# Four blocks of attention: VectorE's share of the exponentials in fewer passes and for more banks, and values without a tick of rest at unit ends

## The chip, the core and the metric

The kernel runs on one core of a Trainium2 chip. The metric is the device time of one execution in microseconds. Five engines take part, each with its own queue of instructions worked off in order: TensorE (PE in the profile, its weight loads PEld), VectorE (DVE), ScalarE (ACT), GpSimd (POOL) and SyncE (SP, which here issues DMAs). They wait for each other through semaphores. Matmuls write to PSUM, eight banks of 128 x 512 float32 values; everything else lies in SBUF or in DRAM.

## The reference

Four transformer blocks follow each other on one sequence of 2048 rows and 640 columns in bf16, with 32 heads of 20 columns. Blocks 1 and 3 use the weights A and a sliding window of 256 keys, causal; blocks 2 and 4 use the weights B and full attention over all 2048 keys, with no mask.

```python
def _B_ref(x, wqkv, wo):                     # full attention; _A_ref adds the window's mask
    qkv = (x @ wqkv) ...                     # 3 x (32 heads, 2048, 20)
    scores = einsum("bhqd,bhkd->bhqk", q, k) * (Dh ** -0.5)
    p = softmax(scores, axis=-1)
    o = einsum("bhqk,bhkd->bhqd", p, v)
    return o.transpose(...).reshape(B, S, D) @ wo

x = x + _A_ref(_layernorm(x), A_wqkv, A_wo)
x = x + _B_ref(_layernorm(x), B_wqkv, B_wo)
x = x + _A_ref(_layernorm(x), A_wqkv, A_wo)
x = x + _B_ref(_layernorm(x), B_wqkv, B_wo)
```

The two full blocks need 2 x 32 x 2048 x 2048 exponentials, the most numerous operation of the kernel.

## The kernel before

The code counts the layers l = 0 to 3. "Layer 2" is l = 1, the first full one; "the last layer" is l = 3.

**Units, banks, ticks.** The work on scores is cut into units: one layer l, one chunk c of 512 queries, one group g of four heads, and for c = 0 of a full layer a part of the keys. A unit of a full layer has 16 blocks of 128 keys for each of its four heads, that is 64 banks: a bank is the scores of one head, 128 keys by 512 queries, and fills one PSUM bank. The loop at the end of the kernel makes one tile of two to four banks in each tick `t`. A tick emits, in this order: the score matmuls of the tile (line 1222), ScalarE's exponential of the whole tile from PSUM to a bf16 tile `pt` in SBUF (line 1253), other work in portions (`pump`), filler matmuls where `keep_clock` finds TensorE too idle (line 613), the value matmuls of banks that were exponentiated two or three ticks earlier (line 1289), a portion of VectorE's own exponentials (`side_step`), and the masks of windowed tiles (line 1325). Even ticks write their scores to PSUM banks 0 to 2, odd ones to 3 to 5, or 3 to 6 when a tile has four banks. Bank 7 (`op`) collects the values of the unit, each of the four heads in 32 of its partitions, and with them the sum of the exponentials in a 21st column. Bank 6 (with 5 at first) is the one bank for all other matmuls: projections, transposes, the output product, the tails.

**Values at a unit's end.** Values are emitted in groups of four banks, one key block for four heads. When the last group of a unit is out, `finish_unit` (line 787) lets VectorE copy bank 7 to `oT` (lines 808 and 810) or to a partial sum `raw_o` (794 and 796); a tail in four steps then normalizes it. The first group of the next unit overwrites bank 7, so it has to wait for that copy. In the kernel before, line 1273 lets no values be emitted in the tick after a unit's end, and allows up to two groups in a later one.

**Exponentials on VectorE.** Some banks of the full layers do not go to ScalarE (`Unit.aside`, line 632): of the last key block, two heads of each unit in layer 2 and four in the last layer, from c = 1 on, with two units left out. VectorE works on them in pairs, by the generator `t_side` (lines 837 to 899). It reads each bank's scores from PSUM and turns them into an integer whose bits are those of 2 to the power of the score (line 858); it splits off the mantissa and the exponent (863, 868, 873), corrects the mantissa by a polynomial of the fourth degree (875 to 893) and multiplies the two (896). Each large pass has 1024 elements for 128 partitions, in float32. `side_step` emits the passes one by one against a credit of 0.65 a tick in layer 2 and 1.05 in the last layer (line 1310). In layer 2 the scores of such a bank take the place of a third bank in a tile, so that ScalarE gets two (line 1137); in the last layer they are an extra matmul to bank 6 (line 851). The values of the pairs are emitted when the unit ends (line 1298, after `side_done`). Intermediate tiles are borrowed: from `raw_o` in layer 2 (`side_early`), from the tiles of normalized inputs in the last layer (`side_start`).

**Other work.** Projections, layer norms, output products and tails are generators with a due unit; `choose` picks the next one and `pump` advances it by a credit of TensorE time. They write to bank 6, have it read by VectorE (line 304 for copies, 539, 995, 1008, 1020), and then give it free for the next tick. When the last layer's chunks c = 1 to 3 are on, only tails and output products are left.

Of the kernel before, what the change touches and what calls it, by code (L numbers as in the profile page):

```python
# [34 lines left out]
EK, ES, EB, EC, ED = (  # L35
    0.34108128280528366, -0.013389613744261132, 0.7155463694844106,
    0.9531181402314826, 0.010462897723623632,
)
# [11 lines left out]
def kernel(  # L50
# [571 lines left out]
    class Unit:  # L622
        def __init__(self, l, c, g, part=None):
# [5 lines left out]
            else:  # L629

                if c > 0 and (l, c, g) not in ((3, 1, 0), (3, NC - 1, G - 1)):
                    self.aside = (2, 3) if l == 1 else (0, 1, 2, 3)
# [3 lines left out]
                    if kc < NT - 1 or j not in self.aside  # L636
                ]
            n = len(sets)
# [179 lines left out]
    def side_start():  # L818

        assert live["xnT"] == 0  # L820
        tl = [xtp.tile([P, KD, C], BF16, name="xnT", tag="xnT") for _ in range(4)]
        live["xnT"] += 4
        f = [v[:, 0:4, :].rearrange("p a b -> p (a b)") for v in tl[0:3]]
        side["tiles"] = [v.bitcast(F32) for v in f] + [tl[3][:, 0:2, :].rearrange("p a b -> p (a b)")]
# [3 lines left out]
    def side_early():  # L828

        b = part_o["t"]  # L830
        side["tiles"] = [b[:, 2 * n : 2 * n + 2, :].rearrange("p a b -> p (a b)") for n in range(3)]
        side["tiles"].append(b[:, 6, :].bitcast(BF16))
        side["out"] = deque([b[:, 7, :].bitcast(BF16).rearrange("p (a b) -> p a b", a=2)])
        side["gen"] = t_side()
        side_step(False)

    def t_side():

        V = nc.vector
        while aside:  # L840
            u = aside[0]
            for pair in range(len(u.aside) // 2):
                while id(u) not in loaded or (u.l == 3 and not side["late"]):
                    yield None
                for i in range(2):
                    yield "bank"
                    xi, xm, xw, xe = side["tiles"]
                    if u.l == 3:
# [3 lines left out]
                            ps[:, 6, :], lhsT=u.k(NT - 1, u.aside[2 * pair + i]),  # L852
                            rhs=u.q(u.aside[2 * pair + i], 0, 4), start=True, stop=True,
# [6 lines left out]
                        scalar1=SCALE * LOG2E * E23, scalar2=127.0 * E23, op0=ALU.mult, op1=ALU.add,  # L860
# [3 lines left out]
                    out=xm.bitcast(I32), in0=xi.bitcast(I32), scalar1=0x7FFFFF, scalar2=0x3F800000,  # L864
# [4 lines left out]
                    out=xi.bitcast(I32), in0=xi.bitcast(I32), scalar1=-0x800000, scalar2=None,  # L869
                    op0=ALU.bitwise_and,  # L870
                )
                yield 0.7
                V.tensor_scalar(out=xe, in0=xi, scalar1=0.0, scalar2=None, op0=ALU.max)
                yield 0.7
                V.tensor_scalar(
                    out=xm, in0=xm, scalar1=EK, scalar2=ES, op0=ALU.mult, op1=ALU.add
                )
                yield 0.7
                V.tensor_tensor(out=xw, in0=xm, in1=xm, op=ALU.mult)
                yield 1.2  # L880
                V.tensor_scalar(out=xw, in0=xw, scalar1=EB, scalar2=None, op0=ALU.add)
                yield 0.7
                V.tensor_tensor(out=xw, in0=xw, in1=xw, op=ALU.mult)
                yield 1.2
                V.tensor_scalar(
                    out=xm, in0=xm, scalar1=EC, scalar2=ED, op0=ALU.mult, op1=ALU.add
                )
                yield 0.7
# [4 lines left out]
                V.tensor_tensor(out=po, in0=xw, in1=xm, op=ALU.add)  # L893
                yield 1.2

                V.tensor_tensor(out=po, in0=po, in1=xe, op=ALU.mult)
                side_out.setdefault(id(u), []).append(pt)
                yield 0.7
# [28 lines left out]
    def side_need(u):  # L927

        if u.l == 3:
            n = 0  # L930
            while u in aside and side.get("scored", {}).get(id(u), 0) < 4:
# [10 lines left out]

    def side_done(u):
        n = 0
        while len(side_out.get(id(u), ())) < len(u.aside) // 2:
# [3 lines left out]
            if side_step(mfree[6][0] <= state["tick"]):  # L949
                continue  # L950
            t = choose(False)
            if t is None:
                state["tick"] += 1
            else:
                advance(t)
        return side_out.pop(id(u))
# [409 lines left out]
```

## Time and profile before

| what | value |
|---|---|
| time, median of 3 runs | 2373.48 us (2369.16 to 2375.21) |
| profiled execution: its own time, its span | 2373.48 us, 2371.8 us |
| busy: TensorE, VectorE, ScalarE, GpSimd | 2015.1, 1459.4, 2183.9, 142.5 us |
| granted TensorE clock, mean | 0.803 |
| exponentials of line 1253 | 1641 activations, 2105.9 us busy |
| score matmuls of line 1222, full layers | 4008, 674.8 us busy |
| value matmuls of line 1289, full layers | 3860, 490.6 us busy |
| VectorE's first read of a bank (line 858) | 88 in the last layer, 48 in layer 2 |

The span is the time from the first to the last instruction. Busy time of an engine counts instructions that overlap once. A matmul's listed duration includes its way through the array, so four matmuls on separate rows or columns of the array, which run at once, are listed with nearly the same start. The names behind an arrow are tiles: `pt<-ps` reads PSUM and writes `pt`. In a table of waits a row gives who waited for whom, microseconds in total, how many times, and the longest.

### The profile page before, as it was taken

What the parts mean: (1) busy time and instruction counts of PE and PEld (TensorE: products, weight loads), DVE (VectorE), ACT (ScalarE), POOL (GpSimd) and SP (SyncE); (2) the same over time, 40 slices, a digit from 0 to 9 for tenths busy, and PEclk for the clock granted to TensorE, in tenths of its full rate; (3) what the DMA queues carried; (4) which work ended last, traced back from release to release, by engine and by line L of the source; (5) the groups of instructions that cost most, each with busy time, mean ns of one, the idle gap of its engine ahead of it and who ended that gap; (6) DMA issues with size and microseconds to landing.
All of it is one profiled execution on the core that took longest, in us unless ns stands there. A gap on an engine that the chain in (4) does not pass through costs nothing.

```text
span 2371.8 us, 39878 instructions
## 1 busy us (share of the span) xinstructions
PE 2015.1 (85%) x15408; PEld 708.8 (30%) x15554; DVE 1459.4 (62%) x2724; ACT 2183.9 (92%) x1753; POOL 142.5 (6%) x295
## 2 busy tenths in 40 slices
PE   7888998878888888888888888888888888888887
PEld 3443333323322332223322333232322222222222
DVE  7676776425646666566666554352577777777772
ACT  7787889898999998999999999999999999999997
POOL 3111110000000001000010011001000000000000
PEclk9998999987987998879997999798655565556556
DMA  6232422322300223102331034022111010001100
GB/s 183 73 101 65 113 68 58 83 62 64 82 19 27 57 54 104 39 14 54 75 89 37 1 87 118 28 42 71 53 32 39 26 38 26 26 26 38 39 14 12
DMA packets 173679, 132.53 MB, mean 56 GB/s; under 512 B 115761, under 2 KB 156081, under 8 KB 173489
## 3 DMA queue, kind: packets, MB, share of 16 engines
q1 hardware_dynamic: 163872, 101.39, 17.3%
q0 software_dynamic: 9616, 28.59, 3.5%
q8 instruction: 122, 2.00, 0.4%
q14 instruction: 69, 0.56, 0.1%
HBM read 98.70 MB, written 27.79 MB: 53 GB/s over the span
## 4 chain that ended last, share of the span: by engine, by line
ACT 35%; PE 33%; issue 14%; DVE 14%; DMA 2%; SPq 2%; POOL 0%; ACTq 0%; DVEq 0%; another core or an unknown queue 0%; POOLq 0%
ACT pt L1253 33%; PE ps L1222 9%; PE ps L1289 6%; PE ps L353 5%; PE ps L530 4%; DVE pt L1325 3%; PE ps L444 3%; PE ps L613 2%; DMA wqk<-in_B_wqkv_dram 1%; DVE st L304 1%; DVE on L1020 1%; ACT ka L1253 1%; DVE oT L810 1%; DVE raw_o L858 1%; PE ps L1016 1%
## 5 line engine op out<-in xcount | busy, mean ns | idle before, releaser
L1253 ACT ACTIVATE pt<-ps 128x1536 bf16<-128x1536 f32 (+2 forms) x1641 | 2105.9, 1451 | 143.6 <-PE ps L1222 129.2
L1222 PE MATMUL ps<-qt,kt 32*128 32x512 bf16 x4008 | 674.8, 480 | 201.9 <-ACT pt L1253 167.9
L1289 PE MATMUL ps<-pt,vt 128*21 128x512 bf16 x3860 | 490.6, 480 | 7.7 <-issue 5.2
L1222 PEld LDWEIGHTS <-kt 32*128 32x128 bf16 x4008 | 190.2, 94 | 648.4 <-issue 627.8
L1325 DVE TENSOR_TENSOR pt<-pt,masks 128x1024 bf16<-128x1024 bf16 (+5 forms) x403 | 239.1, 626 | 134.7 <-ACT pt L1253 134.1
L353 PE MATMUL ps<-xnT,wqk 128*128 128x512 bf16 x760 | 215.6, 395 | 33.2 <-DMA wqk<-in_B_wqkv_dram 11.5
L1289 PEld LDWEIGHTS <-vt 128*21 128x21 bf16 x3960 | 100.7, 91 | 338.5 <-issue 331.1
L304 DVE CAST st<-ps 128x512 bf16<-128x512 f32 x127 | 87.8, 691 | 169.3 <-PE ps L353 165.8
L613 PE MATMUL ps<-masks,ident 128*128 128x512 bf16 x474 | 176.7, 436 | 9.3 <-issue 3.3
L530 PE MATMUL ps<-wop,on 128*128 128x320 bf16 x976 | 171.7, 320 | 6.6 <-DVE on L1020 3.0
L1222 PE MATMUL ps<-qa,ka 32*128 32x384 bf16 (+2 forms) x1408 | 118.9, 279 | 36.1 <-ACT pt L1253 30.5
L858 DVE TENSOR_SCALAR xnT<-ps 128x512 int32<-128x512 f32 x88 | 60.8, 691 | 106.6 <-PE ps L851 103.8
L1020 DVE TENSOR_TENSOR on<-oT,ps 128x512 bf16<-128x512 bf16 x128 | 87.4, 683 | 61.0 <-PE ps L1016 59.6
L810 DVE CAST oT<-ps 128x512 bf16<-128x512 f32 x112 | 76.8, 686 | 73.5 <-PE ps L1289 47.8
L539 DVE TENSOR_TENSOR x_sb<-x_sb,ps 128x320 bf16<-128x320 bf16 x120 | 57.9, 482 | 102.9 <-PE ps L530 102.8
L444 PE MATMUL ps<-wv,xnT 128*128 128x320 bf16 x640 | 111.2, 307 | 8.2 <-DVE va L304 1.8
L530 PEld LDWEIGHTS <-on 128*128 128x128 bf16 x976 | 91.6, 103 | 75.8 <-issue 40.2
L353 PEld LDWEIGHTS <-wqk 128*128 128x128 bf16 x830 | 72.4, 99 | 126.4 <-issue 54.4
L1289 PE MATMUL ps<-pt,va 128*21 128x384 bf16 (+2 forms) x1408 | 81.2, 294 | 6.1 <-DVE pt L1325 2.1
L1222 PEld LDWEIGHTS <-ka 32*128 32x128 bf16 x1408 | 44.7, 92 | 104.4 <-issue 95.2
L444 PEld LDWEIGHTS <-xnT 128*128 128x128 bf16 x640 | 56.6, 99 | 50.3 <-issue 31.6
L1016 PE MATMUL ps<-rT,spread 32*128 32x128 bf16 x512 | 62.0, 254 | 5.2 <-DVE vs L304 2.1
(105 smaller groups left out, 1589.7 us busy)
## 6 DMA issues: line engine op xcount, KB each, us to landing
vt<-v_d SPq DMA_DIRECT2D x48, 336.0 KB
kt<-k_d SPq DMA_DIRECT2D x192, 80.0 KB
wqk<-in_B_wqkv_dram SPq DMA_DIRECT2D x80, 160.0 KB
wqk<-in_A_wqkv_dram SPq DMA_DIRECT2D x70, 160.0 KB
k_d<-st POOLq DMA_DIRECT2D x75, 128.0 KB, 2.2
q_d<-st POOLq DMA_DIRECT2D x75, 128.0 KB, 2.1
qt<-q_d SPq DMA_DIRECT2D x384, 20.0 KB
v_d<-vs POOLq DMA_DIRECT2D x16, 336.0 KB, 3.7
```

Source lines behind the costliest of these rows:

```text
L304: nc.vector.tensor_copy(out=out_, in_=in_)
L353: nc.tensor.matmul(pq, lhsT=wt[:, dc, :], rhs=xt[:, dc, :], start=(dc == 0), stop=(dc == KD - 1),)
L444: nc.tensor.matmul(pv, lhsT=xt[:, dc, i * P : (i + 1) * P], rhs=wv_sb[l % 2][:, dc, h * HD : (h + 1) * HD], start=(dc == 0), stop=(dc == K ...
L530: nc.tensor.matmul(yp, lhsT=on[:, g, qb * P : (qb + 1) * P], rhs=wop[:, g, i * HD : (i + 1) * HD], start=(g == g0), stop=(g == G - 1),)
L613: nc.tensor.matmul(ps[:, b, :], lhsT=ident[:], rhs=masks[:, 0, :], start=True, stop=True)
L810: nc.vector.tensor_copy(out=oT[:], in_=op)
L1016: nc.tensor.matmul(zb[:, qb * P : (qb + 1) * P], lhsT=spread4[:, qb, :], rhs=rT[:], start=True, stop=True,)
L1020: nc.vector.tensor_tensor(out=on[:, g, :], in0=oT[:], in1=zb, op=ALU.mult)
L1222: nc.tensor.matmul(sp[:, i, col * P : (col + qn) * P], lhsT=u.k(kc, j), rhs=u.q(j, q0, qn), start=True, stop=True,)
L1253: nc.scalar.activation(out=pt[:, i:k, b0 * P :], in_=sp[:, i:k, b0 * P :], func=ACT.Exp, scale=SCALE,)
L1289: nc.tensor.matmul(op[32 * j : 32 * j + VW, q0 * P : (q0 + qn) * P], lhsT=u.v(kc, j), rhs=pg[:, i, col * P : (col + qn) * P], start=(first ...
L1325: nc.vector.tensor_tensor(out=pt_[:, i:k, b0 * P :], in0=pt_[:, i:k, b0 * P :], in1=mv_, op=ALU.mult,)
```

## The change

A pair of VectorE's banks takes eight passes in place of twelve: the two reads from PSUM (now scaled and bounded below), two integer passes, and four passes that each do two operations with a second tensor (`scalar_tensor_tensor`), the last of which multiplies with the power of two. The polynomial is of the third degree. Each unit of layer 2 from c = 1 on gives four banks to VectorE instead of two; in the last layer units with an even g give four as before and those with an odd g six. The credit in layer 2 is 0.8 a tick. The values of a pair are emitted with a group of its unit's values, four ticks after the pair's last pass or at the unit's end. `side_step` is called before the values of a tick, not after them. The tick without values after a unit's end and the two groups in one tick are gone: every tick may emit one group. A four-bank tile may follow a use of bank 6 one tick of its kind earlier.

```diff
-                    self.aside = (2, 3) if l == 1 else (0, 1, 2, 3)
+                    self.aside = tuple((NT - 1, j) for j in range(4))
+                    if l == 3 and g % 2:
+                        self.aside += ((NT - 2, 0), (NT - 2, 1))
...
                     V.tensor_scalar(
                         out=xi.bitcast(I32)[:, i * C : (i + 1) * C], in0=side["psum"],
-                        scalar1=SCALE * LOG2E * E23, scalar2=127.0 * E23, op0=ALU.mult, op1=ALU.add,
+                        scalar1=SCALE * LOG2E * E23, scalar2=-128.0 * E23,
+                        op0=ALU.mult, op1=ALU.max,
                     )
                     yield 0.7
                 V.tensor_scalar(
-                    out=xm.bitcast(I32), in0=xi.bitcast(I32), scalar1=0x7FFFFF, scalar2=0x3F800000,
+                    out=xm.bitcast(I32), in0=xi.bitcast(I32), scalar1=0x7FFFFF, scalar2=0x3E800000,
                     op0=ALU.bitwise_and, op1=ALU.bitwise_or,
                 )
...
+                V.scalar_tensor_tensor(
+                    out=xw, in0=xm, scalar=EA, in1=xm, op0=ALU.add, op1=ALU.mult
+                )
                 yield 1.2
+                V.scalar_tensor_tensor(
+                    out=xm, in0=xw, scalar=EB, in1=xm, op0=ALU.mult, op1=ALU.add
+                )
                 yield 1.2
+                V.scalar_tensor_tensor(
+                    out=xw, in0=xw, scalar=EC, in1=xm, op0=ALU.add, op1=ALU.mult
+                )
+                yield 1.2
...
+                V.scalar_tensor_tensor(
+                    out=po, in0=xw, scalar=ED, in1=xi, op0=ALU.add, op1=ALU.mult
+                )
+                side_out.setdefault(id(u), deque()).append(
+                    (u.aside[2 * pair : 2 * pair + 2], pt, state["tick"] + 4)
+                )
                 yield 1.2
...
+    def side_values(u, wait=True):
+
+        done = side_out.get(id(u), ())
+        while done and not (wait and done[0][2] > state["tick"]):
+            which, pt, _ = done.popleft()
+            for n, (kc, j) in enumerate(which):
+                u.left[j] -= 1
+                nc.tensor.matmul(
+                    op[32 * j : 32 * j + VW, :], lhsT=u.v(kc, j), rhs=pt[:, n, :],
+                    start=False, stop=u.left[j] == 0,
+                )
+            valued[id(u)] += len(which)
+            side["out"].append(pt)
...
-            if u.aside and len(at) < 2 and banks[n + 1][0] is u and len(tiles) >= 3 * len(at) + (at or [0])[0]:
+            if (
+                u.aside and len(at) < len(u.aside) and banks[n + 1][0] is u
+                and len(tiles) >= (at or [0])[0] + (0, 2, 10, 12)[len(at)]
+            ):
...
-            if t % 2 and not tails and state["held"] is None and mfree[6][0] < state["tick"]:
+            if t % 2 and not tails and state["held"] is None and mfree[6][0] <= state["tick"]:
...
                 pump(r, r + 0.1)
+                side["credit"] = min(side["credit"] + (SIDE_RATE if side["late"] else 0.8), 1.2)
+                side_step(False)
...
-            for n in range(2 if n_b == 0 or t > closed + 1 else 0):
-                u = pts[0][3][0] if pts else None
-                size = 4
-                if u is not None and u.aside and pts[0][3][4][0][0] == NT - 1:
-                    size -= len(u.aside)
-                if len(pts) < size or pts[size - 1][0] > t - n - (3 if u.windowed else 2):
-                    break
+            u = pts[0][3][0] if pts else None
+            size = 4
+            if u is not None:
+                size -= sum(kc == pts[0][3][4][0][0] for kc, _ in u.aside)
+            if len(pts) >= size and pts[size - 1][0] <= t - (3 if u.windowed else 2):
                 group = [pts.popleft() for _ in range(size)]
...
-                if end and u.aside:
-                    pair = side_done(u)
...
+                if u.aside:
+                    (side_done if end else side_values)(u)
                 if end:
                     pv_emitted(u)
                     finish_unit(u)
-                    closed = t
-                    break
-
-            if n_b:
-                side["credit"] = min(side["credit"] + (SIDE_RATE if side["late"] else 0.65), 1.2)
-                side_step(False)
```

## The prediction

> **What bounds the kernel now.** I read the page first (busy shares and the forty slices), then the table by stretches of time, then the groups by shape, the waits of TensorE in the two stages that the change touches, and last the timeline.
>
> ```profile
> PE 2015.1 (85%) x15408; PEld 708.8 (30%) x15554; DVE 1459.4 (62%) x2724; ACT 2183.9 (92%) x1753; POOL 142.5 (6%) x295
> ...
> PEclk9998999987987998879997999798655565556556
> ...
> ACT 35%; PE 33%; issue 14%; DVE 14%; DMA 2%; SPq 2%; POOL 0%; ACTq 0%; DVEq 0%; another core or an unknown queue 0%; POOLq 0%
> ```
>
> ScalarE is busy 92% of the span, yet the chain that ended last gives it 35% and TensorE 33%: they hand the pace to each other. The granted clock is near full until about 1690 us and near half after.
>
> ```profile
> core 0: us, PE busy (x) PEld busy (x) DVE busy (x) ACT busy (x) POOL busy (x), PEclk, DMA share, GB/s
> 541.00:1400.00 859.00, 732.11 (x5836) 265.82 (x5903) 526.26 (x998) 804.70 (x626) 45.77 (x89) 0.89 0.21 53
> 1400.00:1691.00 291.00, 249.17 (x2006) 91.31 (x2028) 119.34 (x254) 276.60 (x204) 19.94 (x39) 0.88 0.26 63
> 1691.00:2310.00 619.00, 516.86 (x3252) 141.41 (x3251) 472.16 (x687) 603.24 (x442) 0.00 (x0) 0.55 0.11 31
> ```
>
> The first row is the stage with VectorE's early exponentials (layer 2), the last that of the late ones (the last layer). ScalarE idles 54 us in the first and 16 us in the last.
>
> ```profile
> PE ps L1222 <- ACT pt L1253: 61.1, 142, 0.8
> PE ps L408 <- DVE xn L399: 5.5, 8, 2.3
> PE ps L990 <- DVE on L1020: 5.3, 10, 0.9
> ...
> PE ps L1222 <- ACT pt L1253: 79.3, 227, 0.9
> PE ps L1222 <- ACT ka L1253: 15.0, 21, 1.2
> ```
>
> TensorE's waits: three rows of 541 to 1400 us, two of 1691 to 2310. In the last layer it waits 94 of its 102 idle us for ScalarE, so ScalarE sets the pace. In layer 2 it waits 61 us for ScalarE, and all rows there that name VectorE add to 38 us; ScalarE in turn waits 52 us for TensorE there. No engine has room in layer 2.
>
> **ScalarE's part.** The two programs' instruction lists give the activations: 1366 of three banks, 194 of two and 25 of four become 1282, 241 and 47. Seventy banks of 512 leave ScalarE. The price of a bank:
>
> ```profile
> 1846.97 11.19 ACT L1253 ACTIVATE pt<-ps 128x1536 bf16<-128x1536 f32 x8
> 1857.70 2.23 ACT L1253 ACTIVATE ka<-ps 128x2048 bf16<-128x2048 f32 x1
> 1859.45 1.81 ACT L1253 ACTIVATE pt<-ps 128x1536 bf16<-128x1536 f32 x1
> ```
>
> Starts are 10.73 / 8 = 1.341 us apart at three banks and 1.75 at four (the durations overlap), so a bank costs 0.41. Layer 2: 48 activations go from three banks to two, 48 x 0.41 = 19.7 us. Last layer: 36 fewer of 1.341 and one fewer of two banks (0.93), 22 more of 1.75: 48.3 + 0.9 - 38.5 = 10.7. Together 30.4 us of ScalarE's work.
>
> **VectorE's part.** A pair of banks before:
>
> ```profile
> L858 DVE TENSOR_SCALAR xnT<-ps 128x512 int32<-128x512 f32 x88 | 60.8, 691 | 106.6 <-PE ps L851 103.8 <-ACT pt L1253 2.3
> L893 DVE TENSOR_TENSOR ka<-xnT 128x1024 bf16<-128x1024 f32 x44 | 53.8, 1222 | 1.0
> L879 DVE TENSOR_TENSOR xnT<-xnT 128x1024 f32<-128x1024 f32 x44 | 53.7, 1221 | 0.7
> L868 DVE TENSOR_SCALAR xnT<-xnT 128x1024 int32<-128x1024 int32 x44 | 30.5, 694 | 1.5
> ```
>
> Two reads of 0.69, seven passes of about 0.69 and three of 1.22 are 9.88 us. After: two reads, two integer passes of 0.69 and four fused passes. A large fused pass (scalar, then a second tensor) is not in this trace. Its nearest row is the tensor-by-tensor pass over the same 1024 float32, 1.22; the ends are 0.69 (the one-tensor pass) and 2.44 (both halves in turn). I take 1.22, since it too reads two float32 tensors: 2.76 + 4.88 = 7.65 us a pair. Last layer: 44 x 9.88 = 435 becomes 55 x 7.65 = 421, nothing to pay. Layer 2: 24 x 9.88 = 237 becomes 48 x 7.65 = 367, 130 us more on an engine that is 61% busy there; it goes to 77%.
>
> The page "VectorE: DVE Perf Modes" of the Trainium skill, section Rules for kernel authors, speaks against the edit: do not fuse chained operations for speed, only their count matters. By count alone twelve instructions become eight and a pair would cost two thirds, 6.6 us, an estimate; the rows give 7.65, because the float32 passes that remain are of the slow kind.
>
> **What of layer 2's 19.7 us is kept.** Three things stand against it.
> First, a tile with two banks for ScalarE still brings TensorE three score matmuls and a tick's projections. The trace has such tiles already. In its records for this stage an activation ends on average 0.11 us later than it could behind the one before; the two that follow a two-bank one, 0.15 and 0.20. So 0.13 us is lost per tile: 48 x 0.13 = 6.2 (ends 0 and 19.7).
> Second, the evictions of projections, tails and norms queue behind VectorE's passes, and TensorE with its one spare bank (bank 6) queues behind them. The 38 us of such waits stand beside 237 us of exponentials; in proportion, 130 more bring 21. I take half, 10, as TensorE has nearly as much wait for ScalarE (61) as ScalarE for it (52). Ends: 0, if all of it lies in those 61, and 54, if the waits grow with the square of the load and all pass on.
> The third is the order at unit ends.
>
> **Unit ends.** The tick of rest is gone, and of the 160 unit ends some 90 now have one tick between the last values of a unit and the first of the next, by the emitted order; before, all but one had two or more. Those first values overwrite bank 7 and wait for its copy on VectorE. In the timeline a group of values lasts 0.39 to 0.61, the copy 0.69, with 0.1 to 0.2 between: 1.2 to 1.4 us, against a tick of 1.34. At half clock nothing is left to wait; at full clock TensorE's own work in between (group, scores, a filler, some projections) is about 0.9, so 0.37 at most, 33 us over 90. As ScalarE paces most ticks, I take 0.1 us, half of it passed on: 4. Below nothing is possible: two groups in one tick crowd TensorE, and in 300 to 540 us the activations within 1 us of the copies were late by 13.4 us where 6.9 would be their share, so -6. That VectorE's step is now ahead of the copy costs little: it stands directly in front of 37 copies instead of 21, and such steps run ahead of TensorE.
>
> **Last layer.** 22 more side scores at 0.38 each (starts 1851.49 and 1851.87 in the timeline) and 11 more pairs of values are about 13 us of TensorE, under 94 us of waits for ScalarE: 0. If that cover went, 13. Four-bank tiles two ticks after a side score need its read from bank 6 done; 2.7 us against 0.69: 0. The four ticks before a pair's values hide in the six ticks of the next pair's work. DMAs, SyncE's and GpSimd's queues keep their number, and no step is moved past them but by the order of ticks. The 12 fewer filler matmuls (549 to 537) are at most 12 x 0.44 = 5 us of TensorE in layer 2; taken as 0.
>
> The page "TensorE: Matmul & The Clock Gate", Part 1, says that a busy window of about 3.4 us releases the throttle. The row of 1691 to 2310 us has the clock at 0.55 with TensorE busy 83%. By the rule the late matmuls would run at full clock and the cover be larger still; the row decides.
>
> **The sum.** -30.4 + 6.2 + 10 + 4 = -10.2. The profiled execution took 2373.48 with a span of 2371.8; its own time is also the median of the three shown. So a span of about 2361.5 and a time of 2363. A change of 0.3%, 7 us here, is about what can be told from none.
>
> **The rivals.**
> A. Layer 2 gives nothing: its 19.7 us go to the two-bank tiles and the waits behind VectorE, and the last layer's 10.7, less 4 for unit ends, remains: 2367 to 2373. For it: TensorE's time in layer 2 without its waits for ScalarE is 798 us, ScalarE's busy time 805. Against: most two-bank tiles of before are followed without a delay.
> B. VectorE decides layer 2, slower than before. Place: the evictions in front of bank 6 while a pair is in work, which is now nearly all of each full unit. If the 38 us of waits grow with the square of the load (54 more), all passed on: -30.4 + 6.2 + 54 + 4 = +34, 2407; it decides once more than about 20 us of added waits reach ScalarE. For it: ScalarE already waits 52 us for TensorE there. Against: in the last layer VectorE is 76% busy and TensorE waits for it under 5 us.
> C. The fused pass costs 2.44. A pair is 12.5 us, the last layer's pairs 55 x 12.5 = 688 us in a stage of 619: at least 70 us slower, 2440.
> D. TensorE follows everywhere and the catch-up's crowding goes too: -30.4 - 6 = -36, 2337.
>
> **Chances.** The forecast with its better neighbours up to D (2340 to 2366): 0.47. A: 0.25. B: 0.26. C: 0.02. Faster by over 0.3% is the first, 0.47; within, A, 0.25; slower, B and C, 0.28. The forecast's own range is 2348 to 2366; the whole one runs from 2342, near D, to 2393, the middle of B.
>
> **What would show it.** Right: activations 1282, 241 and 47; a fused pass near 1.22; the stretch of layer 2 shorter by 0 to 12 us and the last layer's by 8 to 11; VectorE near 77% in layer 2. TensorE's waits for VectorE there near 60 us. Wrong: those waits above 80 us; a large row of values waiting for the copy (oT, raw_o) from bank 7; a last layer that is not shorter though ScalarE has less to do.

## The result, and the profile after

The changed kernel takes 2431.85 us (median of 4 runs, 2429.67 to 2434.79); the kernel before took 2371.32 beside it (4 runs, 2360.93 to 2375.21). The ratio is 1.026, with an interval of 1.023 to 1.030: slower by 60 us, where 10 us less had been forecast, and outside the range. The profiled execution took 2429.67 us with a span of 2427.9, 56 more than the 2371.8 of before.

Two parts of the page of the changed kernel: busy time of each engine, and the granted clock in forty slices.

```profile
PE 2036.5 (84%) x15395; PEld 701.2 (29%) x15542; DVE 1573.9 (65%) x2732; ACT 2164.7 (89%) x1738; POOL 143.3 (6%) x295
...
PEclk9899999988888998777887789989775565556556
```

ScalarE has 19 us less to do and VectorE 115 more, as planned; yet ScalarE's share of the span falls from 92% to 89%, so it idles longer. The clock is lower in the middle slices, which are layer 2.

The groups of instructions by shape, changed kernel (busy us, mean ns of one | idle before):

```profile
L1274 ACT ACTIVATE pt<-ps 128x1536 bf16<-128x1536 f32 x1282 | 1783.5, 1496 | 167.6 <-PE ps L1243 149.5 <-issue 5.8 <-DVE raw_o L879 4.4
...
L883 DVE SCALAR_TENSOR_TENSOR xnT<-xnT 128x1024 f32<-128x1024 f32 x55 | 67.1, 1220 | 0.8
```

The fused pass takes 1.22 us, and the three-bank activations are 1282. The line numbers have moved: the activation is now line 1274, the score matmuls 1243, the values 1311.

Where the 56 us lie is read between the same unit ends in both traces: VectorE's copies of bank 7 (`finish_unit`), counted from the first unit. Ends 64 to 112 bound the stretch in which layer 2 gives banks to VectorE (units of the windowed layer behind it are woven in; "layer 2" means this stretch from here on), ends 136 to 159 the last layer's. The stretches of the kernel before:

```profile
core 0: us, PE busy (x) PEld busy (x) DVE busy (x) ACT busy (x) POOL busy (x), PEclk, DMA share, GB/s
576.00:1422.00 846.00, 719.38 (x5770) 262.13 (x5834) 515.24 (x981) 795.58 (x619) 46.85 (x91) 0.89 0.22 54
...
1724.00:2359.00 635.00, 528.21 (x3320) 142.82 (x3319) 456.93 (x667) 619.28 (x452) 0.00 (x0) 0.54 0.10 28
```

and those of the changed one:

```profile
577.00:1473.00 896.00, 748.04 (x5760) 262.18 (x5825) 634.97 (x1071) 783.30 (x620) 47.65 (x91) 0.85 0.20 51
...
1773.00:2417.00 644.00, 536.34 (x3332) 135.91 (x3332) 447.29 (x585) 613.38 (x436) 0.00 (x0) 0.56 0.10 28
```

Layer 2 is 50 us longer, the last layer 9 (8 by the exact ends, which the tables below use); the rest gives 3 back. In layer 2 ScalarE's idle time grows from 50 us (846.0 less 795.6) to 113. TensorE issues the same number of matmuls and is busy 29 us longer with them, at a clock of 0.85 instead of 0.89. Here are the largest waits of TensorE in that stretch of the changed kernel (us in total, times, longest):

```profile
PE ps L1243 <- ACT pt L1274: 52.6, 119, 0.9
PE ps L1311 <- DVE oT L814: 16.8, 16, 2.0
PE ps L1009 <- DVE on L1039: 7.9, 13, 1.0
PE ps L405 <- DVE xn L396: 5.8, 9, 1.5
```

ScalarE's largest row there, changed kernel:

```profile
ACT pt L1274 <- PE ps L1243: 103.0, 136, 3.3
```

and in the kernel before:

```profile
ACT pt L1253 <- PE ps L1222: 45.0, 85, 1.8
```

TensorE's second row is new: values waited for the copy of bank 7. All rows that name VectorE add to 40 us before and 72 after; with gaps under 0.15 us, which the rows leave out, it is 44 and 76. ScalarE's waits for scores more than double.

### The profile page after: what moved, and what is told of

It reads as the page before. It is cut to its first block, busy times and chain, and to the rows that moved or that the text cites. A ratio compares the mean times of both kernels' runs of the same rounds, so it can differ in the third digit from the quotient of the medians.

```text
span 2427.9 us, 39817 instructions
## 1 busy us (share of the span) xinstructions
PE 2036.5 (84%) x15395; PEld 701.2 (29%) x15542; DVE 1573.9 (65%) x2732; ACT 2164.7 (89%) x1738; POOL 143.3 (6%) x295
## 5 line engine op out<-in xcount | busy, mean ns | idle before, releaser
L1274 ACT ACTIVATE pt<-ps 128x1536 bf16<-128x1536 f32 (+2 forms) x1604 | 2046.7, 1390 | 218.4 <-PE ps L1243 196.8
L1311 PE MATMUL ps<-pt,vt 128*21 128x512 bf16 x3702 | 476.2, 477 | 37.7 <-DVE oT L814 26.3
L1243 PEld LDWEIGHTS <-kt 32*128 32x128 bf16 x3986 | 178.6, 95 | 619.0 <-issue 600.9
L610 PE MATMUL ps<-masks,ident 128*128 128x512 bf16 x461 | 169.3, 429 | 10.4 <-issue 3.3
L863 DVE TENSOR_SCALAR xnT<-ps 128x512 int32<-128x512 f32 x110 | 76.1, 692 | 150.3 <-PE ps L857 140.8
L441 PE MATMUL ps<-wv,xnT 128*128 128x320 bf16 x640 | 116.8, 319 | 10.5 <-DVE va L301 2.3
L863 DVE TENSOR_SCALAR raw_o<-ps 128x512 int32<-128x512 f32 x96 | 66.1, 688 | 68.2 <-PE ps L1243 64.3
L1274 ACT ACTIVATE ka<-ps 128x2048 bf16<-128x2048 f32 x47 | 90.4, 1923 | 0.2 <-PE ps L1243 0.2
```

Of the source, the lines that this page charges most:

```text
L441: nc.tensor.matmul(pv, lhsT=xt[:, dc, i * P : (i + 1) * P], rhs=wv_sb[l % 2][:, dc, h * HD : (h + 1) * HD], start=(dc == 0), stop=(dc == K ...
L610: nc.tensor.matmul(ps[:, b, :], lhsT=ident[:], rhs=masks[:, 0, :], start=True, stop=True)
L863: V.tensor_scalar(out=xi.bitcast(I32)[:, i * C : (i + 1) * C], in0=side["psum"], scalar1=SCALE * LOG2E * E23, scalar2=-128.0 * E23, op0=AL ...
L1243: nc.tensor.matmul(sp[:, i, col * P : (col + qn) * P], lhsT=u.k(kc, j), rhs=u.q(j, q0, qn), start=True, stop=True,)
L1274: nc.scalar.activation(out=pt[:, i:k, b0 * P :], in_=sp[:, i:k, b0 * P :], func=ACT.Exp, scale=SCALE,)
L1311: nc.tensor.matmul(op[32 * j : 32 * j + VW, q0 * P : (q0 + qn) * P], lhsT=u.v(kc, j), rhs=pg[:, i, col * P : (col + qn) * P], start=(first ...
```

## The experiments

The first question was which part costs the 60 us. The theories were: the order at unit ends (U for the missing tick of rest, P for VectorE's passes ahead of the copy); VectorE's load in layer 2 (V); the two-bank tiles themselves (T: TensorE doesn't follow a tick of 0.92 us); and the filler matmuls, which are counted by ScalarE's banks and so become fewer when a tile has two (K). Ratios are against the kernel before on the same chip, with 95% intervals; by these intervals the difference of two runs is uncertain by some 7 to 12 us, and by 4 where both were timed ten times or more.

**Parts taken out of the changed kernel.** `two_in_layer2`: two banks a unit in layer 2, as before the change.

```diff
-                    self.aside = tuple((NT - 1, j) for j in range(4))
+                    self.aside = tuple((NT - 1, j) for j in ((2, 3) if l == 1 else range(4)))
```

> The changed kernel with two banks a unit for VectorE in layer 2 again (heads 2 and 3), all else as changed. The changed kernel is 60 us slower than before, 51 of it gained between the first and the last unit of layer 2. All theories that put the cause into layer 2's extra banks (V: evictions wait behind VectorE's passes; K: more two-bank tiles, the clock falls) expect about 45 us back, near 2387 us. U (the first values of a unit wait for the copy of bank 7, because the tick of rest is gone) expects at most 15 back, 2417 or more.

`rest_tick`: the tick without values after a unit's end is back, with up to two groups in a later one.

```diff
-            if len(pts) >= size and pts[size - 1][0] <= t - (3 if u.windowed else 2):
+            for n in range(2 if n_b == 0 or t > closed + 1 else 0):
...
+                if len(pts) < size or pts[size - 1][0] > t - n - (3 if u.windowed else 2):
+                    break
...
                     finish_unit(u)
+                    closed = t
+                    break
```

> The changed kernel with the tick of rest after a unit's end and the catch-up of two groups restored, all else as changed. U expects at least the 26 us of TensorE's waits for the copy oT back, and up to 60: 2372 to 2405. V and K expect under 10 us: 2422 or more.

`rest_and_step_last`: the tick of rest, and VectorE's step behind the values of its tick.

```diff
                 pump(r, r + 0.1)
-                side["credit"] = min(side["credit"] + (SIDE_RATE if side["late"] else 0.8), 1.2)
-                side_step(False)
...
                     finish_unit(u)
...
+            if n_b:
+                side["credit"] = min(side["credit"] + (SIDE_RATE if side["late"] else 0.8), 1.2)
+                side_step(False)
```

> The changed kernel with the tick of rest restored and VectorE's step put back behind the values of a tick. With the tick of rest alone it took 2419 us. P (the step ahead of the values puts passes in front of the copy of bank 7 and of the masks) expects 10 to 25 us less than that, 2394 to 2409. V (evictions behind more passes in layer 2) and K (two-bank tiles and the clock) expect the same 2419, give or take 5.

`heat_of_three`: a tile of two banks for ScalarE and one for VectorE counts as three for the fillers (`n_s` counts all of a tile's banks).

```diff
-                state["heat"] += 0.414 * n_b
+                state["heat"] += 0.414 * n_s
...
-                    keep_clock(1.0 * n_b - surplus)
+                    keep_clock(1.0 * n_s - surplus)
```

> The changed kernel with the tile's third bank, the one for VectorE, counted in the sum that decides on filler matmuls, so that a two-bank tile is kept as busy as one of three. K expects the clock in layer 2 to rise from 0.84 to about 0.89 and 20 to 45 us back. V expects no gain, or up to 10 us lost, since TensorE has more to do. U expects no change.

`short_in_layer2`: two of the four fused passes are left out there, so that VectorE's values in layer 2 are no longer the exponentials.

```diff
-                V.scalar_tensor_tensor(
-                    out=xm, in0=xw, scalar=EB, in1=xm, op0=ALU.mult, op1=ALU.add
-                )
-                yield 1.2
-                V.scalar_tensor_tensor(
-                    out=xw, in0=xw, scalar=EC, in1=xm, op0=ALU.add, op1=ALU.mult
-                )
-                yield 1.2
+                if u.l == 3:
+                    V.scalar_tensor_tensor(
+                        out=xm, in0=xw, scalar=EB, in1=xm, op0=ALU.mult, op1=ALU.add
+                    )
+                    yield 1.2
+                    V.scalar_tensor_tensor(
+                        out=xw, in0=xw, scalar=EC, in1=xm, op0=ALU.add, op1=ALU.mult
+                    )
+                    yield 1.2
```

> The changed kernel without two of the four fused passes of each pair in layer 2, so that a part of the polynomial is left out there: a pair costs 5.2 us instead of 7.65 and VectorE's exponentials in layer 2 come to 250 us, near the 237 of before, at the same number of banks. V expects 35 us or more back, 2397 or less. K and U expect under 10 us, 2422 or more.

| run | median us | ratio | layer 2, us | last layer, us |
|---|---|---|---|---|
| before | 2371.32 | 1 | 846 | 635 |
| changed | 2431.85 | 1.026 [1.023, 1.030] | 897 | 643 |
| two_in_layer2 | 2410.74 | 1.017 [1.015, 1.020] | 872 | 644 |
| rest_tick | 2419.24 | 1.020 [1.018, 1.023] | 894 | 638 |
| rest_and_step_last | 2410.64 | 1.017 [1.016, 1.019] | 885 | 640 |
| heat_of_three | 2424.69 | 1.024 [1.021, 1.028] | 887 | 643 |
| short_in_layer2 | 2409.62 | 1.017 [1.014, 1.019] | 866 | 643 |

No single part explains it: `two_in_layer2`, `rest_tick`, `rest_and_step_last` and `short_in_layer2` all fell between the ranges that the theories gave. The order at unit ends, both halves together, is worth 21 us; the second pair in layer 2 another 21; half of its fused passes 22 (each give or take 10); the fillers 7, which is not told from nothing.

**Parts put alone on the kernel before.** `fused_alone` has the eight passes and their constants, as in the diff of the change, and nothing else. `no_rest_alone` allows one group of values in every tick:

```diff
-            for n in range(2 if n_b == 0 or t > closed + 1 else 0):
+            for n in range(1):
```

`step_first_alone` moves the two lines of the credit and `side_step` up behind `pump`, at the old credit of 0.65.

> The kernel before with the passes of the changed kernel alone: eight of 7.65 us a pair for twelve of 9.88, the same banks, the same credit, values at the unit's end. V by load expects 0 to 10 us less than before, 2361 to 2371, as VectorE has 53 us less to do in layer 2 and 98 in the last layer. L (what counts is how long a single pass stands in front of an eviction: four of 1.22 in place of three) expects the same or up to 15 us more, to 2386.

> The kernel before without the tick of rest and with one group of values a tick, nothing else. U (first values wait for the copy of bank 7) expects 8 to 20 us more than before, 2379 to 2391. If the tick of rest matters only beside VectorE's larger load, under 5 us more.

> The kernel before with VectorE's step put ahead of a tick's values, nothing else. P expects 8 to 25 us more than before, 2379 to 2396. V, K and U expect no change, within 4 us.

They took 2369.97, 2378.66 and 2366.40 us: ratios 1.000 [0.999, 1.002], 1.003 [1.000, 1.005] and 1.000 [0.998, 1.002]. VectorE had 141 us less to do in the first (1318.5 busy against 1459.4), and the time did not move. By the ratios the two order changes cost 7 (1 to 12) and 0 alone; taking both back from the changed kernel gave 21. TensorE's waits for the copy `oT`, over the whole span, say the same: 0.4 us before, 15 without the rest, 4.5 with the step first, 35 in the changed kernel. Their product shows in the timeline of the changed kernel, where the copy `oT` (line 814) has to wait for two integer passes that `side_step` put ahead of it (start us, us, engine, line):

```profile
1247.79 0.69 DVE L869 TENSOR_SCALAR raw_o<-raw_o 128x1024 int32<-128x1024 int32 x1
1248.51 0.69 DVE L874 TENSOR_SCALAR raw_o<-raw_o 128x1024 int32<-128x1024 int32 x1
1249.12 0.68 DVE L814 CAST oT<-ps 128x512 bf16<-128x512 f32 x1
...
1249.85 0.61 PE L1311 MATMUL ps<-pt,vt 128*21 128x512 bf16 x4 [1.69 <-DVE oT L814]
...
1251.10 1.45 ACT L1274 ACTIVATE pt<-ps 128x1536 bf16<-128x1536 f32 x1 [2.14 <-PE ps L1243]
```

The next unit's values come one tick after the last ones, and stand 1.69 us behind the copy; the next scores are behind them in TensorE's queue, and ScalarE stands 2.14 us. With the tick of rest and the step behind the values no wait for that copy is left in either stretch.

**What remains in layer 2.** On top of `rest_and_step_last` (+41 us against before), each with the edit that is shown above under its namesake: `rs_two`, two banks in layer 2; `rs_heat`, fillers by three banks; `rs_short`, two fused passes less in layer 2 (again not the exponentials). `rs_two_last4` has two banks in layer 2 and four in every unit of the last layer, as before the change.

> The changed kernel with the tick of rest and VectorE's step behind the values (together 2411 us), and two banks a unit in layer 2. If the extra banks of layer 2 are what remains there, it falls by the 39 us that the units of layer 2 are still longer than before: 2372 to 2380. If the denser credit of 0.8 a tick or the values four ticks later cost by themselves, 2385 to 2395.

> The changed kernel with the tick of rest and VectorE's step behind the values, and with the third bank of a tile counted for the filler matmuls. K (TensorE's clock falls because a two-bank tile is filled up less) expects 15 to 35 us less than 2411 and a clock in layer 2 of 0.90 or more. V expects 2405 to 2415.

> The changed kernel with the tick of rest and VectorE's step behind the values, and without two of the four fused passes of a pair in layer 2 (a part of the polynomial is left out there). V (evictions wait behind passes) expects 20 to 35 us less than 2411, down to 2376. K expects 2400 or more, as the two-bank tiles are all there.

> As the one with two banks a unit in layer 2, and also four banks in every unit of the last layer: the numbers of banks of the kernel before. What is left of the change is the fused passes, the values of a pair four ticks later and the credit of 0.8. Expected from the runs of single parts: 2365 to 2375. If the six banks of the odd units in the last layer are a gain of ScalarE's 10.7 us, it is slower than its sister by 5 to 11; if they cost, as the last layer 8 us longer than before says, it is faster by 5 to 10.

They took 2395.38 (1.011 [1.007, 1.016]), 2415.23 (1.019 [1.017, 1.022]), 2405.66 (1.015 [1.012, 1.018]) and 2391.76 (1.009 [1.006, 1.011]). So with the unit ends in order the second pair still costs 15 us (give or take 11; layer 2 of the traces is 885 us long with it and 870 without): it takes 20 us of work from ScalarE and costs 35 elsewhere. The fillers are out. The length of the passes is worth 5 here, not told from nothing, so most of the 22 of `short_in_layer2` is gone once the unit ends are in order. The two extra banks in the last layer are worth nothing: four are better by 4, inside the uncertainty.

But `rs_two_last4`, expected at 2365 to 2375, has as many banks on VectorE as the kernel before, with shorter passes, and is still 21 us slower. Three small differences are left, and each was turned back by itself. `u_credit` sets the credit in layer 2 from 0.8 to 0.65. `u_offset` puts the two short tiles of a unit at distance 3, where the kernel before has them:

```diff
-                and len(tiles) >= (at or [0])[0] + (0, 2, 10, 12)[len(at)]
+                and len(tiles) >= (at or [0])[0] + (0, 3, 10, 13)[len(at)]
```

`u_values` emits the pairs' values at the unit's end only:

```diff
                 if u.aside:
-                    (side_done if end else side_values)(u)
+                    if end:
+                        side_done(u)
```

> The version with the bank counts of before, the tick of rest and the step behind the values took 2392 us, 20 more than before, though fused passes alone cost nothing. Three things are left of the change in layer 2; this one puts the credit back from 0.8 to 0.65 a tick. If the denser passes cost (C), 2370 to 2380. Otherwise 2388 to 2396.

> The same version with the credit of 0.8 and VectorE's banks of layer 2 three tiles apart (0, 3) instead of two (0, 2), as before. If TensorE can't follow two short tiles with one between them (O), 2370 to 2380: ScalarE was late above all three to eight tiles after a pair's start. Otherwise 2388 to 2396.

> The same version with a pair's values at the unit's end alone, as before, instead of four ticks after its last pass. If the two extra matmuls in the middle of a unit, which leave half of the array idle, cost (E), 2375 to 2385. Otherwise 2388 to 2396.

The result is 2385.99 (1.006 [1.004, 1.008]), 2377.74 (1.003 [1.002, 1.004]) and 2390.74 (1.007 [1.005, 1.010]): 6, 14 and 1 us less; the 14 alone is clear of the uncertainty (7). One number, 2 for 3 in the place of a short tile, carries some 14 of the 60 us. What it does is seen at one and the same unit end in the two traces. With distance 2:

```profile
765.79 0.23 PE L1023 MATMUL ps<-ident,hl 128*32 128x128 bf16 x1
...
766.20 0.68 DVE L867 TENSOR_SCALAR raw_o<-raw_o 128x1024 int32<-128x1024 int32 x1
766.92 0.69 DVE L872 TENSOR_SCALAR raw_o<-raw_o 128x1024 int32<-128x1024 int32 x1
767.53 0.20 DVE L1025 COPY rT<-ps 32x128 bf16<-32x128 bf16 x1
...
767.79 1.01 PE L610 MATMUL ps<-masks,ident 128*128 128x512 bf16 x2 [1.44 <-DVE rT L1025]
```

With distance 3:

```profile
770.66 0.23 PE L1023 MATMUL ps<-ident,hl 128*32 128x128 bf16 x1
...
771.07 0.68 DVE L861 TENSOR_SCALAR raw_o<-ps 128x512 int32<-128x512 f32 x1
...
771.67 0.20 DVE L1025 COPY rT<-ps 32x128 bf16<-32x128 bf16 x1
...
771.92 0.38 PE L610 MATMUL ps<-masks,ident 128*128 128x512 bf16 x1 [0.33 <-DVE rT L1025]
```

The tail of the unit before reads PSUM in short copies (`rz`, 0.25 us; `rT`, 0.20), each with a step of TensorE waiting behind it. At distance 2 the second bank is read a tick earlier, and both integer passes, 1.37 us together, stand ahead of `rT`; at distance 3 one read does. Counted over layer 2, TensorE stands 0.8 us or longer behind `rz` or `rT` 16 times in `rs_two_last4` and 5 times in `u_offset` (and 5 times in the kernel before).

**Why such a stall may cost more than its length.** After the stall of 1.44 us above, two filler matmuls take 1.01 us; two that start at 764.71, before it, take 0.61. Around the first stall the granted clock was 0.88 from 764.5 to 767 us and 0.50 from 768 to 775, and ScalarE was busy 5.1 of these 7 us. The records of the granted clock in layer 2 know two values, 1.0 and 0.5, in steps of 3.4 us. In all 20 traces together, TensorE stood 336 times at least 0.8 us for VectorE in layer 2 while the clock was full. A stretch at half clock began within 4 us of the start of 206 of these stalls, 61%. After stalls of 0.5 to 0.8 us it was 25% (103 of 415), after those of 0.2 to 0.5 us 12% (89 of 735), which is also what chance would give (the stretches' starts, 4 us each, cover 12% of the time at full clock). The shortest that the rows count, 0.15 to 0.2 us, are out of line: 21 of 71. And a long stall behind VectorE is not the only way in: it stands within 4 us ahead of 196 of the 399 stretches. The changed kernel in one such stretch, and before and after it:

```profile
1034.00:1058.00 24.00, 19.61 (x177) 6.78 (x180) 13.97 (x21) 23.78 (x20) 0.00 (x0) 1.00 0.11 32
1058.00:1089.00 31.00, 28.43 (x182) 8.02 (x178) 20.93 (x35) 23.62 (x19) 0.00 (x0) 0.50 0.00 1
1089.00:1102.00 13.00, 10.64 (x91) 4.61 (x92) 10.14 (x18) 13.00 (x11) 0.00 (x0) 1.00 0.17 50
```

At full clock ScalarE is busy throughout. At 0.50 TensorE is busy 92% and ScalarE 76%: TensorE sets the pace there. Page "TensorE: Matmul & The Clock Gate" of the Trainium skill, Part 1, has a busy window of about 3.4 us release the throttle. The first and third row agree with two clocks; the second does not agree with the release, if busy is what this trace counts as busy: its 31 us, by estimate nine such windows, hold TensorE 92% busy at half clock.

The waits, the long stalls and the time at half clock go with layer 2's length from run to run. From the traces' records, between unit ends 64 and 112 (waits with the gaps under 0.15 us):

| run | layer 2, us | waits for VectorE, us | of 0.8 us or more | at half clock, us |
|---|---|---|---|---|
| fused_alone | 842 | 50 | 15 | 140 |
| before | 846 | 44 | 12 | 181 |
| u_offset | 856 | 55 | 11 | 174 |
| u_credit | 864 | 57 | 22 | 188 |
| rs_two | 870 | 60 | 23 | 201 |
| rs_short | 877 | 57 | 24 | 253 |
| rest_and_step_last | 885 | 72 | 32 | 249 |
| rest_tick | 894 | 68 | 27 | 287 |
| changed | 897 | 76 | 26 | 276 |

Over all traces but that of `rs_wide` (below; 15 long stalls, 311 us at half clock), layer 2's time goes with the number of long stalls (correlation 0.90), with the time at half clock (0.94), and just as well with the plain sum of the waits for VectorE (0.90). That stalls come ahead of the stretches is shown by the order in time; that they cause them is the likeliest reading, and no run changed the clock alone.

**Whether ScalarE still sets the pace, and other places.** `rs_wide` is `rest_and_step_last` with ScalarE exponentiating the third bank of each short tile as well, unused: 96 tiles x 0.41 = 39 us more work.

```diff
-                        out=pt[:, i:k, b0 * P :], in_=sp[:, i:k, b0 * P :],
+                        out=pt[:, i:k2, b0 * P :], in_=sp[:, i:k2, b0 * P :],
```

`rs_offset` is `rest_and_step_last` with the short tiles at 0, 3, 10 and 13.

> The changed kernel with the tick of rest and the step behind the values (2411 us), in which ScalarE also exponentiates the third bank of each short tile of layer 2, for nothing: the result is not used, VectorE does its four banks a unit as well. ScalarE's work is back to 96 banks more than with the short tiles, 39 us. If ScalarE paces layer 2, as the sum took it, the time rises by 25 to 39, to 2436 to 2450. If TensorE paces the ticks with VectorE's banks (T: the same score matmuls, projections and evictions have to pass in each, however short ScalarE's part is), the time rises by under 12, 2423 or less.

> The changed kernel with the tick of rest and the step behind the values (2411 us), and with VectorE's four banks of a layer 2 unit at the tiles 0, 3, 10, 13 instead of 0, 2, 10, 12. O expects twice the saving of one pair, 2375 to 2395; C and E expect no change, 2406 to 2416.

They took 2449.68 (1.034 [1.032, 1.036]) and 2419.24 (1.020 [1.018, 1.022]): 39 and 9 us more than `rest_and_step_last`. The 39 is just ScalarE's added work, but it does not settle the question. The run added a wait as well: ScalarE's activations of the stretch 573 to 1495 us now stand behind VectorE's read of the same bank (last column, idle before).

```profile
L1277 ACT ACTIVATE pt<-ps 128x1536 bf16<-128x1536 f32 x579 | 796.8, 1471 | 101.4 <-DVE raw_o L863 61.2 <-PE ps L1244 35.7 <-PE ps L1035 1.4
```

The traces of before and after say more about T. An activation is called late by the time that it ended behind the one before, less the shortest such interval of its size; in layer 2 this adds to some 67 us before and 136 after. Of the 69 us more, 36 are activations with a wait of TensorE for VectorE (0.15 us or longer) in the 3 us ahead of them, 30 are activations at half clock without one, and 4 are at full clock without one. So at full clock the added two-bank tiles by themselves cost little; how much of the 30 is theirs, and how much the clock's, is open.

`rs_offset` is a miss: what gives 14 us with two banks gives nothing with four (9 us more, 7 by the ratios, give or take 7). The long stalls were 27 against 32, but at other places (10 behind `on` instead of 8, 3 behind `rT` instead of 10), and the time at half clock was 283 us against 249. Why is open; a pair from tile 13 leaves fewer ticks to the unit's end, but that was not tried.

**The best parts together.** `mixed`: fused passes, tick of rest, step behind the values, two banks in layer 2 at distance 3 with credit 0.65, and six banks in the last layer's odd units but for the last of these.

```diff
+                    if l == 3 and g % 2 and (c, g) != (NC - 1, G - 3):
+                        self.aside += ((NT - 2, 0), (NT - 2, 1))
```

> The parts that cost nothing or gained alone: fused passes, the tick of rest, the step behind the values, layer 2 with two banks a unit three tiles apart and the credit of 0.65, values four ticks later, and six banks in the odd units of the last layer but for its last odd unit, where a stall of 4 us for the third pair was seen. The last layer should then keep 4 to 8 of ScalarE's 10.7 us: 2363 to 2372. If ScalarE's gain there goes to TensorE's waits, 2372 to 2378.

2375.79 against 2371.19, 1.002 [1.001, 1.003], with layer 2 at 850 and the last layer at 636. No version tried beats the kernel before; its last layer, 635, is not shortened by six banks even where the unit ends are in order.

## Why the prediction was wrong

**Right.** The counts of activations, the fused pass at 1.22 us, VectorE's load (120 us more in layer 2, where 130 were forecast; 71% of the longer stretch, not 77%) and ScalarE's work (measured as busy time, 12.3 us less in layer 2 and 5.9 in the last layer; by the counts and the distance of starts 20 and 11) came as said. So did two of the marks named for a wrong forecast: a row of values waiting for the copy, and a last layer that is not shorter. The third, waits for VectorE above 80 us, did not come: they were 72.

**"What of layer 2's 19.7 us is kept", 6.2 + 10.** This is the term that failed most. The activations were late by 69 us more, as said above; less the 20 of work, these are the 50 us. Even with the unit ends in order (`rest_and_step_last`) layer 2 is 39 us longer at 20 us less work: 59 lost, where 16 had been put. The prediction priced VectorE's added queue by the sum of TensorE's waits (38 in its stretch, to "near 60"; 40 became 72) and halved what is added, as if a wait cost half its length. That price is what failed: 32 us of added waits went with 69 us of lateness. Long stalls doubled from 12 to 26, and time at half clock rose from 181 to 276 us; the sum of waits follows layer 2's length as closely as the count of long stalls does, so the runs don't show that the sum was the wrong thing to count. Lateness of ScalarE, by the clock at an activation's end, was some 0.07 us per us at full clock and 0.13 at half clock before; after, 0.12 and 0.23. The forecast's words that "TensorE has nearly as much wait for ScalarE (61) as ScalarE for it (52)" hold at full clock only: of TensorE's waits for ScalarE, 1.9 us lay in the half-clock time, in both traces. There was no cover there. (The 52 is 49 by the rows of waits, which changes nothing.)

**The place of the short tiles** was in the diff and on no line of the sum. It costs 14 us with two banks (give or take 7), and with it passes come in front of the tail's copies.

**"Unit ends", 4.** Some 21 were measured for rest and step together. The step that failed is "That VectorE's step is now ahead of the copy costs little": alone it does cost nothing, as the prediction would have it, but with the rest gone too, a copy behind two passes had a group of values waiting. Each was priced as if the other had not been made.

**"Last layer", 10.7 us for nothing paid.** It became 9 us longer. ScalarE's idle time rose from 16 us (635.0 less 619.3) to 31. The waits of TensorE in that stretch of the changed kernel:

```profile
PE ps L1243 <- ACT pt L1274: 46.2, 126, 0.9
PE ps L1243 <- ACT ka L1274: 32.9, 43, 1.2
PE ps L1311 <- DVE oT L814: 12.0, 16, 1.8
PE ps L955 <- DVE ka L895: 4.7, 2, 4.0
```

12 us are the copies again, and 4.0 one stall at the end of the last unit with six banks, whose third pair wasn't ready: ScalarE stands as long. In `rest_and_step_last` the copy's row is gone and 640 us are left; in `mixed` the stall too, and 636 are left. There ScalarE is late in ticks at half clock that bring the score of a VectorE bank (line 857) or the values of a pair, as in this tick of `mixed`, at clock 0.50:

```profile
2115.01 0.61 PE L1244 MATMUL ps<-qt,kt 32*128 32x512 bf16 x3
...
2115.69 0.58 PE L857 MATMUL ps<-qt,kt 32*128 32x512 bf16 x1
...
2116.20 0.61 PE L1312 MATMUL ps<-pt,vt 128*21 128x512 bf16 x4
...
2116.74 1.18 PE L1244 MATMUL ps<-qt,kt 32*128 32x512 bf16 x6
...
2117.46 1.45 ACT L1275 ACTIVATE pt<-ps 128x1536 bf16<-128x1536 f32 x1 [0.20 <-PE ps L1244]
```

From scores to scores are 1.73 us, where an activation needs 1.34. In ticks without output products the late activations of the last layer add to 1 us in the kernel before and 8 in `mixed`, nearly all of these in ticks with such a score or such values; in ticks with output products they add to 17 and 21. The 11 us more use up ScalarE's gain of some 10. So the step that failed is the sentence on the added side scores and values, "about 13 us of TensorE, under 94 us of waits for ScalarE: 0": the waits are real as a sum, but they don't lie in the ticks where this work falls. ("If that cover went, 13" was near.)

**The rivals.** B had the direction and the place, waits behind VectorE in layer 2, at +34 against the measured +60; TensorE's added waits were 32 us, past its threshold of 20. But waits that grow in sum are not the whole: the unit ends, the place of the tiles and the last layer have their own shares, and the waits came with more time at half clock. C is out by the 1.22 (its 2.44 was not the two halves in turn either: by the rows these are 0.69 and 1.22, 1.91), A and D by the sign.

**The page that spoke against the edit.** "VectorE: DVE Perf Modes" of the Trainium skill, Rules for kernel authors, advises not to fuse chained operations for speed, and to keep their number small. Fewer passes are cheaper here, 141 us of VectorE in `fused_alone`, which agrees with the second half (a part of it is the polynomial's lower degree, not the fusing). That the time did not move says nothing on the first half, since VectorE's total set nothing.

In steps from the changed kernel back, the 60 us are: tick of rest 13, step behind the values 9, second pair of layer 2 15, extra banks of the last layer 4, distance of the short tiles 14. The 4 can't be told from nothing, and the others are larger than their uncertainty of 7 to 11 us by little. The 7 us that `u_offset` still lies above the kernel before are the credit (6 by itself, which may overlap the distance) and what can't be told apart.

## What to carry to other kernels

Price more work on an engine off the path by what it will stand in front of: list the short copies and evictions that the pacing engines wait for, and see in the emitted order how many passes come ahead of each, for every shift of one tick. Where the granted clock falls after idle time, don't take a wait at its own length: look at the long stalls beside the sum, and look for cover in the half-clock ticks, and in the ticks where the added work falls, separately. Price parts that meet at the same instruction together: two changes of order that cost 7 and 0 alone were worth 21 when both were taken back.

## What the runs showed of the hardware

- In layer 2, with TensorE busy some 84%, the granted clock changes between 1.0 and 0.5 in stretches at half clock of 3 to 34 us, and 61% of the stalls behind VectorE of 0.8 us or more at full clock (206 of 336) are followed by one within 4 us, against 12% by chance. TensorE's longest wait in this stretch of the changed kernel is 2.3 us, with 25 stretches at half clock.
- Exponentials from PSUM that follow each other end 0.91, 1.34 and 1.77 us apart at the least for two, three and four banks, though one lasts 1.05, 1.50 and 1.92 (means of the changed kernel).
- A `scalar_tensor_tensor` over 1024 float32 a partition takes 1.22 us, no more than a `tensor_tensor` of that size.
